# Four first expert blocks instead of three, three of them by seven products

## The chip, the cores and the metric

The kernel runs on one core of a Trainium2 chip. The metric is the device time of one execution in microseconds (us). Three runs of the kernel before gave 645.27, 646.94 and 648.63 us, so the median is 646.94 us. The profile is one further execution.

The engines are TensorE (PE in the profile, its weight loads PEld), VectorE (DVE), ScalarE (ACT), GpSimd (POOL) and SyncE (SP). SP issues the large loads, POOL the gathers and scatters by index.

## The reference

Attention with a causal sliding window of 64 over 8 sequences of 576 tokens, 8 heads of 64, is followed by a mixture of 8 experts with one expert per token:

```python
# x: attention output, (B, S, D) = (8, 576, 512); E = 8 experts; F = 1024
logits = x @ w_gate;  local = sigmoid(x @ w_local)
for b in range(B):
    prev = -1
    for s in range(S):
        fresh = argmax(logits[b, s])
        e = fresh if s == 0 or local[b, s] < 0.5 else prev
        prev = e
        p = softmax(logits[b, s])
        h = relu(x[b, s] @ w1[e])
        out[b, s] = p[e] * (h @ w2[e])
```

A token may take over the expert of the token before it, so the expert of a token is known only once the sequence has been scanned up to it.

## The kernel before, in words

**Attention** (`attention`, L167) goes through 9 chunks of 512 tokens (`sc`), each with 4 pairs of heads (`hp`): 36 units, written (sc, hp) here. A unit's scores (L377) are made two units ahead on PE, ACT takes the exponential (L415), and DVE multiplies by a mask (L420), but for the units in `BIASED`, where PE adds the mask as a bias. `values` (L423) multiplies with V on PE, and DVE scales (L440). The chunks 4 to 8 (`GATED`) get their gate logits beside the values. Each finished chunk is written to `xs` in DRAM by POOL (L532). Inside attention, PE, ACT and SP execute in the order in which the code is written; DVE's and POOL's order comes from a planner.

**Routing** (`Router`) works in two parts. The first (`first`, L986) takes the tokens up to `T1` = 3 sequences, finds each token's expert, and places tokens of full groups of 256 with one expert into `FB` = 3 first blocks. The second (`second`, L1019) takes the rest and builds the table of all further blocks. Both are generators, woven into other work: each `yield` gives a weight (the DVE work just written, in us) and a flag `trip`, which says that the next piece starts on PE with what DVE or ACT has just made. In attention a local `step` runs twice per unit and goes on when the weights, paid off at `HALF` per step, allow it. In the expert stage another `step` (L1441) pays off `STEP` = 3.5 per call.

The table (L938) is built from one-hot matrices, ten chunks of 128 tokens at a time: `one` and `colh` on DVE, `rowh` (in the second part) on ACT by an absolute value for each chunk (L964) and one relu (L966), then bfloat16 matmuls on PE (L972). The result gives the indices `gx` for the gathers. `weigh` (L883) writes each token's probability into a column of `xs` by DMAs on SP.

**Experts** (`Experts`) processes blocks of 256 tokens with one expert each, named -1, -2, -3 for the first blocks and 0, 1, ... for the further ones, with some smaller blocks between. Per block: a gather of rows (`rows`, L1130, on POOL), a load of `w1` and `w2` (`weights`, L1154, 2 MB each, on SP, into a ring of four buffers that attention's loads share), the transpose (`turn`, L1170), `hidden` and `result`. Blocks named in `PLAIN` (-1 and -2) use plain matmuls (L1375, L1407). All other large blocks use seven products in place of eight for each of the two matrix multiplications (`big_hidden` L1216, `big_result` L1268), for which DVE first makes sums of quarters: `xs` and `ws1` of input and `w1` (in `prepare`), `ws2` of `w2`, `hs` of the hidden layer. In such a block some results are read from a bank of PSUM that a later product adds into, so that product waits for the reader.

`run` (L1426) sets the order. PE and SP go in program order through the expert stage; DVE and ACT are left to the planner until block -3 is reached (L1481). Before block -3 the generator of the second part is emptied (L1476), the flag is made (L1479), and the next blocks are fetched by the new table.

Of the kernel before, what the change touches and what calls it, by code (L numbers as in the profile page):

```python
# [19 lines left out]
P = 128  # L20
# [6 lines left out]
N = B * S  # L27
# [9 lines left out]
T1 = 3 * S  # L37
CUT = T1 % P
PART = slice(0, T1 // P + 1), slice(T1 // P, C)
C1 = PART[0].stop  # L40
CV = C + 1
CMAX = max(p.stop - p.start for p in PART)
FB = 3
FIRST = 2 * FB
assert CUT and CUT % 32 == 0
# [10 lines left out]
ZR = 16 * P  # L56
# [13 lines left out]
HALF = 0.8  # L70
STEP = 3.5
LEAD = 2
MID = (KB, KB - 1)
PLAIN = (-1, -2)
# [92 lines left out]
def attention(ctx, tc, ring, kq, v3, v4, vt, vh, xs, lt, ok, wg, wg2, ident, rt, ex):  # L167
# [302 lines left out]
    for i, (sc, hp) in enumerate(units):  # L470
# [27 lines left out]
        if side is None and 4 * sc >= C1 and hp >= 2:  # L498
            side = rt.first(bank)
# [198 lines left out]
class Router:  # L698
# [18 lines left out]
    def prepare(self):  # L717
        nc = self.nc
        tl, iota = self.tl, self.iota
        self.io8 = iota("io8", [P, 1, E], [[0, 1], [1, E]])  # L720
        self.io8m = tl("io8m", P, 1, E)
        nc.vector.tensor_scalar(self.io8m, self.io8, -float(E), None, Alu.add)
        self.io128 = iota("io128", [P, 1, P], [[0, 1], [1, P]])
        self.ios = iota("ios", [P, 1, NS], [[0, 1], [1, NS]])
        self.iob = iota("iob", [1, NBLK, 1], [[1, NBLK], [0, 1]])
        pos = iota("pos", [P, G, GC], [[0, G], [P, GC]], 1)
        self.ones = tl("ones", P, P)
        nc.vector.memset(self.ones, 1.0)
        self.tri = tl("tri", P, P)
        nc.gpsimd.affine_select(out=self.tri, in_=self.ones, compare_op=Alu.is_gt, fill=0.0, base=0,  # L730
                                pattern=[[1, P]], channel_multiplier=-1)
        self.zero = tl("zero", P, CMAX * E)
        nc.vector.memset(self.zero, 0.0)
        self.begin = tl("begin", P, C)
        begin2 = tl("begin2", P, C)
        posf = pos.rearrange("p g c -> p (g c)")
        nc.vector.tensor_scalar(self.begin, posf, 0.0, None, Alu.is_equal)
        nc.vector.tensor_scalar(begin2, posf, float(S), None, Alu.is_equal)
        nc.vector.tensor_tensor(self.begin, self.begin, begin2, op=Alu.add)
        self.oh, self.rank = tl("oh", P, CV, E), tl("rank", P, CV, E)  # L740

        self.chunk = tl("chunk", P, CV, dt=BF16)
        for i, a in enumerate((0, C1)):
            c = PART[i]
            n = c.stop - c.start
            nc.vector.tensor_copy(self.chunk[:, a:a + n], iota(f"chunk{i}", [P, n], [[1, n]], 0, c.start - C))
        self.at = iota("posp", [P, 1], [[0, 1]], 1)
        self.cnt = [tl("cnt0", P, E), tl("cnt1", P, E)]
        self.lim1 = tl("lim1", P, E)
# [19 lines left out]
    def gate(self, part, psum):  # L769
# [75 lines left out]
        vec.memset(oh[:CUT, 0, :] if part else oh[CUT:, n - 1, :], 0.0)  # L845
# [37 lines left out]
    def weigh(self, part):  # L883

        chunks, xs = PART[part], self.xs
        c = chunks.start
        for a, b in ((0, T1), ) if not part else ((T1, ZR), (ZR, N)):
            for a, b in ((a, -(-a // P) * P), (-(-a // P) * P, b // P * P), (b // P * P, b)):
                if a >= b:
                    continue  # L890
                i, n, p = a // P, max(1, (b - a) // P), min(P, b - a)
                self.nc.sync.dma_start(
                    out=xs[row_of(a):row_of(a) + b - a, D:].rearrange("(c p) o -> p c o", p=p),
                    in_=self.pt[a % P:a % P + p, i - c:i - c + n])
# [7 lines left out]
    def places(self, pl, n):  # L902

        vec = self.nc.vector

        def tl(name, p, n, dt=F32):
            return self.tl(name, p, CV, dt=dt)[:, :n]

        plc = tl("plc", P, n)
        vec.tensor_reduce(plc, pl, axis=AX.X, op=Alu.add)  # L910

        vec.memset(plc[CUT:, C1 - 1:C1], float(2 * N))
        if n > C1:
            vec.memset(plc[:CUT, C1:C1 + 1], float(2 * N))
        plc_i = tl("plc_i", P, n, dt=I32)
        vec.tensor_copy(plc_i, plc)
        lo_i = tl("lo_i", P, n, dt=I32)
        vec.tensor_scalar(lo_i, plc_i, P - 1, None, Alu.bitwise_and)
        vec.tensor_scalar(plc_i, plc_i, P.bit_length() - 1, None, Alu.arith_shift_right)
        lo, hi = tl("lo", P, n), tl("hi", P, n)  # L920
        vec.tensor_copy(lo, lo_i)
        vec.tensor_copy(hi, plc_i)
        return lo, hi
# [14 lines left out]
    def table(self, psum, cs, ns, lo, hi, idx, gx):  # L938
# [5 lines left out]
        for k in range(0, len(pieces), 2):  # L944
            built = []
            for b, m in pieces[k:k + 2]:
# [15 lines left out]
                if ns != FIRST:  # L962
                    for i in range(m):
                        nc.scalar.activation(rowh[:, i, :], self.io128[:, 0, :], Act.Abs, bias=lo[:, b + i:b + i + 1],  # L964
                                             scale=-1.0)
                    nc.scalar.activation(rowh, rowh, Act.Relu, bias=self.ones[:, :1], scale=-1.0)  # L966
                yield 0.6 if ns == FIRST else 0.42 * m, (b, m) in (pieces[-1], pieces[k + 1:k + 2] and pieces[k + 1])
# [18 lines left out]
    def first(self, psum):  # L986
# [18 lines left out]
        pl = tl("pl", P, CV, E)[:, :C1]  # L1005
# [13 lines left out]
    def second(self, psum):  # L1019
# [55 lines left out]
        CE = [P, CV, E]  # L1075
# [16 lines left out]
        lo, hi = self.places(pl, CV)  # L1092
# [9 lines left out]
        at = yield from self.table(psum, slice(0, CV), NS, lo, hi, tabs["idx"], tabs["gx"])  # L1102
# [14 lines left out]
class Experts:  # L1117
# [52 lines left out]
    def turn(self, st, quiet, later=False):  # L1170
# [12 lines left out]
        if st["fast"] and not quiet and not later:  # L1183
            self.prepare(st)

    def prepare(self, st):

        st["xq"] = quarters(st["xt"], DK, BIG)
        st["xt"] = self.right("xs", st["xq"])
# [3 lines left out]
        st["ws"] = self.left("ws1", st["wq"])  # L1193

    def left(self, name, a):

        sub, add = Alu.subtract, Alu.add
        s1, s2, s3, s4 = self.sums(name, a)
        for o, x, y, op in ((s1, a[1][0], a[1][1], add), (s2, s1, a[0][0], sub), (s3, a[0][0], a[1][0], sub),
                            (s4, a[0][1], s2, sub)):  # L1200
            self.nc.vector.tensor_tensor(o, x, y, op=op)
        return s1, s2, s3, s4

    def right(self, name, b):

        sub = Alu.subtract
        t1, t2, t3, t4 = self.sums(name, b)
        for o, x, y in ((t1, b[0][1], b[0][0]), (t2, b[1][1], t1), (t3, b[1][1], b[0][1]), (t4, b[1][0], t2)):
            self.nc.vector.tensor_tensor(o, x, y, op=sub)
        return t1, t2, t3, t4  # L1210
# [5 lines left out]
    def big_hidden(self, st):  # L1216
# [9 lines left out]
        st["w2t"] = self.right("ws2", w2)  # L1226
# [22 lines left out]

        product(px, a[0][0], b[0][0], stop=False)  # L1250
        u = keep(0, px)
        product(py, s[0], t[0], stop=False)
        z = keep(1, py)
        product(px, s[1], t[1], False, False)
        v = keep(2, px)
        product(pz, a[0][1], b[1][0])
        relu(hq[0][0], pz, u)
        product(px, s[2], t[2], False, False)
        relu(hq[1][1], px, z)
        product(py, s[3], b[1][1], False)  # L1260
        relu(hq[0][1], py, v)
        product(px, a[1][1], t[3], False)
# [3 lines left out]
        st["hs"] = self.left("hs", st["ha"])  # L1266
# [94 lines left out]
    def hidden(self, st, quiet, step):  # L1361
        nc = self.nc
        if st["fast"]:
            return self.big_hidden(st)
# [3 lines left out]
        for g in range(FK // each):  # L1368
            hp = self.ps_h.tile([P, each, n], F32, name="hp")
            for i in range(each):  # L1370
                m = g * each + i
                for kk in range(DK):
                    for f in range(0, P, st["rows"]):
                        a = slice(f, f + st["rows"])
                        nc.tensor.matmul(hp[a, i, :], lhsT=st["w1"][:, kk, m * P:(m + 1) * P][:, a],  # L1375
                                         rhs=st["xt"][:, kk, :n], start=(kk == 0), stop=(kk == DK - 1))
            o = h[:, g * each:(g + 1) * each, :n]
# [4 lines left out]
            step()  # L1382

    def result(self, st, step, hooks=()):
# [3 lines left out]
        if "half" in st:  # L1388
# [13 lines left out]
            step()  # L1402
            return
        for i, s in enumerate(st["slots"]):
            yp = self.ps_y.tile([P, D], F32, name="yp")
            for m in range(FK):
                nc.tensor.matmul(yp, lhsT=st["h"][:, m, i * P:(i + 1) * P], rhs=st["w2"][:, m, :],  # L1407
                                 start=(m == 0), stop=(m == FK - 1))
                if m == FK // 2 - 1:
# [16 lines left out]
    def run(self, ctx, rt, last=None):  # L1426
# [4 lines left out]
        ctx.enter_context(tc.manual_schedule(engines={ET.PE, ET.SP}))  # L1431
# [7 lines left out]
        pause = 0.0  # L1439

        def step():  # L1441
            nonlocal side, pause
            pause -= STEP
            if pause > 0.0:
                return
            pause, trip = 0.6, False
            while side and not trip:
                w, trip = next(side, (0.0, None))
                pause += w
                if trip is None:  # L1450
                    side = None

# [18 lines left out]
        step()  # L1471
        pause += 2.0
        for i, n in enumerate(order):
            quiet = i < FB
            if i == FB - 1:
                while side:  # L1476
                    step()
                if last:
                    last(psum())  # L1479

                ctx.enter_context(tc.manual_schedule(engines={ET.PE, ET.SP, ET.DVE, ET.Activation}))  # L1481
                jobs.append(self.fetch(order[FB]))
                if jobs[i]["fast"]:
                    self.prepare(jobs[i])
# [4 lines left out]
            self.hidden(jobs[i], quiet, step)  # L1489
            if i + 1 == len(order):  # L1490
                self.result(jobs[i], step)
                continue
            self.turn(jobs[i + 1], i + 1 < FB)
            hooks = ()
            if order[i + 1] >= KINDS[2]:
                one, turned, two = self.quarter(jobs[i + 1])
                after = jobs[i + 2]
                hooks = one, turned, two, (lambda: None), (lambda: self.turn(after, False, True)), \
                    (lambda: self.prepare(after))
            self.result(jobs[i], step, hooks)  # L1500

    def more(self, ctx):

        self.space(ctx)
        for n in [*range(SURE[0], NB), *range(NB + SURE[1], NB + E), *range(KINDS[1] + SURE[2], KINDS[1] + E)]:
            st = self.fetch(n)
            self.turn(st, False)
            self.hidden(st, False, lambda: None)
            self.result(st, lambda: None)
# [54 lines left out]
```

## Time and profile before

| what | value |
|---|---|
| median of three runs | 646.94 us |
| profiled execution: time / span | 650.13 / 648.4 us |
| PE busy | 620.2 us (96%) |
| DVE / ACT / POOL busy | 386.3 / 199.9 / 130.7 us |
| attention | 0 to about 136 us |
| blocks -1 and -2, plain | 135.9 to 197.1 us |
| block -3, by seven products | 197.1 to 222.65 us |
| moved by DMA | 166.43 MB, mean 257 GB/s |

A line of the timeline has the start, the length, the engine, the line of the code, the operation, what it writes and reads, its shapes and its count; in brackets stands the idle time before it and what ended that. Neighbours of one kind are merged. A line of the table by windows has, for each engine, the busy time and the number of instructions. Matmul ends are modelled. PE's rows in fp32 count two records for each matmul that the code writes.

### The profile page before, as it was taken

The page shows a single profiled execution, that of the slowest core. Times are in us where ns is not written, and L with a number is a line of the kernel's source. Part 1 is how long each engine was busy: PE and PEld are TensorE (multiplying, and loading weights), DVE is VectorE, ACT ScalarE, POOL GpSimd, SP SyncE. Part 2 cuts the span into 40 slices and gives each one's busy share as a digit, 9 for nine tenths or more (in the row PEclk, how much of TensorE's full clock was granted, in tenths as well). Part 3 has the DMA queues.
Part 4 walks back from the last instruction along what each step waited for, and adds up shares of the span by engine and source line. Part 5 has one row for each costly group of instructions (what it writes and reads, how often), then busy time and mean ns, then how long its engine had stood idle before and what let it go on. Part 6 is the DMA issues. An engine that isn't in the chain of part 4 may idle for free. (4 is left out here: it accounts for less than half of the span.)

```text
span 648.4 us, 14791 instructions
## 1 busy us (share of the span) xinstructions
PE 620.2 (96%) x6319; PEld 536.8 (83%) x6319; DVE 386.3 (60%) x730; ACT 199.9 (31%) x364; POOL 130.7 (20%) x132
## 2 busy tenths in 40 slices
PE   8888997889999999999999999999999999999995
PEld 7777776775759999978998999887997998899994
DVE  6676578753964865364563683362917752886730
ACT  3766755611473122113120312021211221213120
POOL 5422112320002202111302220211312022111101
PEclk9999989999999999999999999999999999999999
DMA  8989999968745655586957565769768456856501
GB/s 331 418 340 343 379 351 370 362 212 361 212 146 213 231 225 187 197 314 253 381 215 259 226 235 221 251 238 365 252 248 317 167 204 251 342 172 231 192 17 38
DMA packets 26725, 166.43 MB, mean 257 GB/s; under 512 B 8163, under 2 KB 9209, under 8 KB 16666
## 3 DMA queue, kind: packets, MB, share of 16 engines
q1 hardware_dynamic: 17802, 135.53, 57.3%
q0 software_dynamic: 8848, 29.85, 11.8%
q8 instruction: 52, 0.85, 0.5%
q14 instruction: 23, 0.19, 0.1%
HBM read 146.18 MB, written 19.59 MB: 256 GB/s over the span
## 5 line engine op out<-in xcount | busy, mean ns | idle before, releaser
L1357 POOL DMA_INDIRECT out_dram<-y,idx x36 | 41.1, 1140 | 347.0 <-DVE y L1293 165.9
L1236 PE MATMUL hp<-xs,ws 128*128 128x128 f32 x672 | 79.6, 275 | 0.0
L1284 PE MATMUL hp<-ws,hs 128*128 128x256 f32 x336 | 77.6, 380 | 0.0
L1236 PEld LDWEIGHTS hp<-xs,ws 128*128 128x128 f32 x672 | 77.3, 192 | 0.0
L1284 PEld LDWEIGHTS hp<-ws,hs 128*128 128x128 f32 x336 | 63.5, 190 | 9.3 <-issue 0.8
L1375 PE MATMUL hp<-xt,w 128*64 128x64 f32 (+2 forms) x640 | 66.3, 276 | 0.9 <-issue 0.9
L1375 PEld LDWEIGHTS hp<-xt,w 128*128 128x128 f32 (+1 forms) x640 | 61.2, 170 | 5.9 <-issue 2.5
L1293 DVE SCALAR_TENSOR_TENSOR y<-hp,xg,kept 128x256 f32<-128x256 f32 x42 | 19.7, 481 | 71.4 <-issue 47.0
L1247 DVE TENSOR_TENSOR h<-hp,keep 128x512 f32<-128x512 f32 x42 | 28.7, 690 | 53.3 <-PE hp L1236 53.3
L1147 POOL DMA_INDIRECT xg<-xs,gx x40 | 48.7, 1217 | 44.7 <-issue 37.8
L1407 PE MATMUL yp<-w,h 128*128 128x512 f32 x128 | 56.6, 593 | 0.0
L1236 PEld LDWEIGHTS hp<-xt,w 128*128 128x128 f32 x448 | 53.2, 192 | 2.7 <-issue 1.3
L1236 PE MATMUL hp<-xt,w 128*128 128x128 f32 x448 | 54.7, 275 | 0.0
L1284 PE MATMUL hp<-w,h 128*128 128x256 f32 x224 | 53.6, 382 | 0.0
L430 PE MATMUL xo<-vb,p 128*64 128x74 f32 (+1 forms) x576 | 44.7, 230 | 8.5 <-issue 4.1
L415 ACT ACTIVATE p<-sp 128x512 f32<-128x512 f32 x72 | 39.2, 595 | 39.4 <-PE sp L384 37.3
L384 PEld LDWEIGHTS sp<-w 64*64 64x64 f32 x1296 | 38.7, 137 | 13.2 <-issue 9.9
L430 PEld LDWEIGHTS xo<-vb,p 128*64 128x64 f32 x576 | 39.0, 139 | 10.9 <-issue 4.8
L420 DVE TENSOR_TENSOR p<-p,mask 128x1024 f32<-128x1024 f32 x29 | 35.7, 1231 | 19.9 <-ACT p L415 19.8
L384 PE MATMUL sp<-w 64*64 64x128 f32 (+1 forms) x1296 | 43.7, 268 | 3.5 <-issue 2.4
L1284 PEld LDWEIGHTS hp<-w,h 128*128 128x128 f32 x224 | 41.3, 190 | 5.6 <-issue 0.4
L430 PE MATMUL xo<-va,p 128*64 128x74 f32 (+1 forms) x576 | 44.7, 230 | 0.8 <-issue 0.8
(280 smaller groups left out, 935.7 us busy)
## 6 DMA issues: line engine op xcount, KB each, us to landing
w<-in_w_dram SPq DMA_DIRECT2D x48, 2048.0 KB, 10.1
w<-in_kq_dram SPq DMA_DIRECT2D x17, 1024.0 KB, 10.4
xs<-x POOLq DMA_DIRECT2D x9, 1024.0 KB
va<-in_v_dram SPq DMA_DIRECT2D x5, 1184.0 KB
vtt<-in_vt_dram SPq DMA_DIRECT2D x5, 1024.0 KB, 6.8
va<-in_v_dram SPq DMA_DIRECT2D x3, 1040.0 KB, 8.9
va<-in_v_dram SPq DMA_DIRECT2D x2, 520.0 KB, 6.9
w<-in_kq_dram SPq DMA_DIRECT2D x2, 512.0 KB, 3.7
```

The source lines that it names most:

```text
L384: nc.tensor.matmul(sp[j][c * WIN:(c + 1) * WIN, a:b], lhsT=kt[h, hp, block * WIN:(block + 1) * WIN], rhs=qt[h, hp, a:b], start=not biased, ...
L415: nc.scalar.activation(p[:, j], sp[j], Act.Exp, scale=DH ** -0.5)
L420: masked.append(nc.vector.tensor_tensor(p, p, m.to_broadcast([P, 2, SC]), op=Alu.mult))
L430: nc.tensor.matmul(xo[par * WIN:(par + 1) * WIN, j, s * VW:s * VW + n], lhsT=p[:, j, b * WIN:(b + 1) * WIN], rhs=w[:, s, 2 * hp + j, :n], ...
L1147: self.nc.gpsimd.indirect_dma_start(out=x, out_offset=None, in_=self.xs[:rows, :], in_offset=bass.IndirectOffsetOnAxis(ap=gx[:, s:s + 1], ...
L1236: nc.tensor.matmul(out[:, m, :], lhsT=a[:, kk, m * P:(m + 1) * P], rhs=b[:, kk, :], start=start and m + kk == 0, stop=stop and (m, kk) == ...
L1247: nc.vector.tensor_tensor(o, x, y, op=add)
L1284: nc.tensor.matmul(out, lhsT=a[:, m, :], rhs=b[:, m, :], start=start and m == 0, stop=stop and m == FK // 2 - 1, skip_group_check=True)
L1293: nc.vector.scalar_tensor_tensor(y[i][:, j * w:(j + 1) * w], x, pw[i], y2, Alu.mult, Alu.add)
L1357: self.nc.gpsimd.indirect_dma_start(out=self.out[:, :], out_offset=bass.IndirectOffsetOnAxis(ap=st["idx"][:, s:s + 1], axis=0), in_=y, in_ ...
L1375: nc.tensor.matmul(hp[a, i, :], lhsT=st["w1"][:, kk, m * P:(m + 1) * P][:, a], rhs=st["xt"][:, kk, :n], start=(kk == 0), stop=(kk == DK - 1))
L1407: nc.tensor.matmul(yp, lhsT=st["h"][:, m, i * P:(i + 1) * P], rhs=st["w2"][:, m, :], start=(m == 0), stop=(m == FK - 1))
```

## The change

The first part of routing takes four sequences (2304 tokens, 18 whole chunks of 128), so that no chunk is shared by the two parts and the code for a shared chunk goes. There are four first blocks, and only -1 is plain; 12 further large blocks are certain instead of 13. The first part's generator starts once chunk 5 has begun, and attention's `step` pays off 1.0 instead of 0.8.

In the expert stage PE, SP, DVE and ACT are all in program order from the start. The generator of the second part now tells DVE work and ACT work apart and yields in smaller pieces, and `step(room)` pays off both: 1.7 and 1.7 per step in the plain block's hidden layer, 0.9 and 1.7 in its result, 0.5 and 1.4 in the blocks by seven products. The sums of the next block and of `w2` are handed out a few at a time at the same places. The generator is emptied before block -4.

```diff
-T1 = 3 * S
-CUT = T1 % P
-PART = slice(0, T1 // P + 1), slice(T1 // P, C)
+T1 = 4 * S
+PART = slice(0, T1 // P), slice(T1 // P, C)
-CV = C + 1
-FB = 3
+FB = 4
-ZR = 16 * P
+ZR = 20 * P
-HALF = 0.8
-STEP = 3.5
+HALF = 1.0
+HALFWAY, BESIDE, WITHIN = (1.7, 1.7), (0.9, 1.7), (0.5, 1.4)
-PLAIN = (-1, -2)
+PLAIN = (-1,)
...
-        if side is None and 4 * sc >= C1 and hp >= 2:
+        if side is None and 4 * sc >= C1 and (hp >= 2 or sc - 1 in GATED):
             side = rt.first(bank)
...
-                if ns != FIRST:
-                    for i in range(m):
-                        nc.scalar.activation(rowh[:, i, :], self.io128[:, 0, :], Act.Abs, bias=lo[:, b + i:b + i + 1],
-                                             scale=-1.0)
-                    nc.scalar.activation(rowh, rowh, Act.Relu, bias=self.ones[:, :1], scale=-1.0)
-                yield 0.6 if ns == FIRST else 0.42 * m, (b, m) in (pieces[-1], pieces[k + 1:k + 2] and pieces[k + 1])
+                trip = (b, m) in (pieces[-1], pieces[k + 1:k + 2] and pieces[k + 1])
+                if ns == FIRST:
+                    yield 0.6, trip
+                    continue
+                yield 0.17 * m, False
+                for i in range(m):
+                    nc.scalar.activation(rowh[:, i, :], self.io128[:, 0, :], Act.Abs, bias=lo[:, b + i:b + i + 1],
+                                         scale=-1.0)
+                    if i % 4 == 3:
+                        yield 0.0, False, 1.2
+                c = m // 2
+                nc.scalar.activation(rowh[:, :c], rowh[:, :c], Act.Relu, bias=self.ones[:, :1], scale=-1.0)
+                yield 0.0, False, 0.3 * (m % 4) + 0.7
+                nc.scalar.activation(rowh[:, c:], rowh[:, c:], Act.Relu, bias=self.ones[:, :1], scale=-1.0)
+                yield 0.0, trip, 0.7
...
+        def after():
+            if step:
+                self.do(more, 1)
+                step()
+        if not step:
+            self.do(more)
         product(px, a[0][0], b[0][0], stop=False)
         u = keep(0, px)
+        after()
         product(py, s[0], t[0], stop=False)
         z = keep(1, py)
+        after()
...
-        ctx.enter_context(tc.manual_schedule(engines={ET.PE, ET.SP}))
+        ctx.enter_context(tc.manual_schedule(engines={ET.PE, ET.SP, ET.DVE, ET.Activation}))
...
-        def step():
-            nonlocal side, pause
-            pause -= STEP
-            if pause > 0.0:
-                return
-            pause, trip = 0.6, False
-            while side and not trip:
-                w, trip = next(side, (0.0, None))
-                pause += w
+        def step(room):
+            nonlocal side, vector, scalar
+            vector, scalar = max(vector - room[0], -room[0]), max(scalar - room[1], -room[1])
+            while side and vector <= 0.0 and scalar <= 0.0:
+                w, trip, *busy = next(side, (0.0, None))
+                vector, scalar = vector + w, scalar + sum(busy)
                 if trip is None:
                     side = None
+                elif trip:
+                    vector += 0.3
+                    break
...
             if i == FB - 1:
                 while side:
-                    step()
+                    step(HALFWAY)
                 if last:
                     last(psum())
-                ctx.enter_context(tc.manual_schedule(engines={ET.PE, ET.SP, ET.DVE, ET.Activation}))
                 jobs.append(self.fetch(order[FB]))
...
-            self.hidden(jobs[i], quiet, step)
+            self.hidden(st, first, (lambda: step(WITHIN if st["fast"] else HALFWAY)) if i < FB - 1 else None)
...
-            self.turn(jobs[i + 1], i + 1 < FB)
+            after = jobs[i + 1]
+            self.turn(after, i + 1 < FB)
+            if i < FB - 1:
+                def beside():
+                    self.do(after["sums"], 2 if st["fast"] else 1)
+                    step(WITHIN if st["fast"] else BESIDE)
+                self.result(st, beside, [beside] * 6)
+                self.do(after["sums"])
+                continue
```

`do(terms, n)` writes the next `n` of a block's sums; `result` of a plain block calls its `step` four times per half, that of a block by seven products the six hooks between its products.

## The prediction

> **What bounds the kernel now.** I read the page first, then the stage table by windows, then the timelines of TensorE (PE), ScalarE (ACT), VectorE (DVE) and SyncE (SP) around the first expert blocks.
>
> ```profile
> PE 620.2 (96%) x6319; PEld 536.8 (83%) x6319; DVE 386.3 (60%) x730; ACT 199.9 (31%) x364; POOL 130.7 (20%) x132
> ```
>
> PE is busy 96% of the span, so a saving in matmuls counts, and so does every microsecond for which PE has to stand still. By stage (columns: window, then busy us and count of PE, PEld, DVE, ACT, POOL, then granted clock, DMA share, GB/s):
>
> ```profile
> 87.40:105.70 18.30, 15.74 (x398) 13.16 (x401) 15.71 (x62) 10.19 (x18) 3.16 (x3) 0.96 0.97 368
> 105.70:117.00 11.30, 9.86 (x258) 8.03 (x251) 8.14 (x20) 6.08 (x12) 3.27 (x3) 1.00 0.92 305
> 117.00:129.00 12.00, 11.20 (x302) 9.42 (x300) 9.95 (x24) 7.25 (x14) 4.07 (x3) 1.00 1.02 404
> ...
> 136.00:166.00 30.00, 30.00 (x114) 19.86 (x115) 14.63 (x68) 4.51 (x8) 5.76 (x6) 1.00 0.77 290
> 166.00:197.00 31.00, 30.64 (x142) 20.74 (x140) 23.88 (x64) 20.69 (x50) 2.58 (x3) 1.00 0.54 163
> 197.00:222.50 25.50, 25.50 (x177) 24.08 (x178) 15.45 (x34) 5.67 (x10) 5.20 (x6) 1.00 0.60 221
> ```
>
> Attention ends at 136. Two plain blocks follow (136 to 197), then fast blocks of 25.5 us. PE is never idle there, although DVE and ACT do the second routing part beside it. How it ends:
>
> ```profile
> 188.72 7.09 PE L1407 MATMUL yp<-w,h 128*128 128x512 f32 x16
> 195.65 0.99 PE L972 MATMUL r<-colh,rowh 128*128 128x108 bf16 x17
> 197.00 0.27 PE L160 MATMUL r<-ident,ok 128*1 128x128 f32 x1 [0.36 <-DVE t L974]
> 197.11 2.02 PE L1236 MATMUL hp<-xt,w 128*128 128x128 f32 x16
> ```
>
> PE passes from the second plain block to the third block in 1.46 us (195.65 to 197.11), as ACT had made the last one-hot rows beside the block's second result half:
>
> ```profile
> 188.54 3.31 ACT L964 ACTIVATE rowh<-io,lo 128x128 bf16<-128x128 f32 x11
> 191.75 1.35 ACT L966 ACTIVATE rowh<-rowh,ones 128x1280 bf16<-128x1280 bf16 x1
> 193.01 1.84 ACT L964 ACTIVATE rowh<-io,lo 128x128 bf16<-128x128 f32 x6
> 194.88 1.04 ACT L966 ACTIVATE rowh<-rowh,ones 128x896 bf16<-128x896 bf16 x1
> 195.85 0.69 ACT L1412 ACTIVATE y<-yp,xg 128x512 f32<-128x512 f32 x1
> ```
>
> The code writes these rows ahead of that half, so the block's last `y` (195.85) stands behind them and PE's wait is for a few matmuls alone.
>
> **The change part by part.** *Block -2 by seven products.* Sixteen large blocks remain (3 + 13 before, 4 + 12 after); one plain block becomes fast. Plain, from the PE timeline: hidden 13.81 (166.20 to 180.01), turn 0.87, results 6.87 and 6.93: 28.48. Fast: seven hidden products of 1.787, turn 0.87, seven result products of 1.726: 25.46. Gain **-3.0**.
>
> *The metering of the second part.* I walked the generator by its own weights. In the plain block every step pays off 1.7 or 0.9 us of DVE work, in blocks -2 and -3 only 0.5 (24 steps). The 7.2 chunk goes out at the seventh hidden step of block -1, the 7.4 chunk at its fifth result step, the first piece of the table only at the fourth result step of block -2. A piece then costs 1.7 of DVE at 0.5 per step and 4.1 of ACT at 1.4 per step, about six steps in turn; fifteen are left for four pieces. So at block -4 the loop that empties the generator still has: the ten rows of piece 3 on ACT, all of piece 4 (six rows), and the table's end.
>
> *The flush.* PE and ACT now go in program order. PE has the matmuls of pieces 3 and 4 and the transpose of `flag` ahead of block -4; ACT has block -3's last `y` ahead of the rows, and that waits for PE's last product. From that product's end: `y` 0.72 (starts 0.25 late, runs 0.47, as at 222.90), ten rows at 0.30 (eleven took 3.31) 3.0, two half activations of 640, 0.75 each (from 1.35 for 1280 and 1.04 for 896, overlap taken off) 1.5, six rows 1.8, two halves of 384 1.1: 8.1. Then six matmuls, the copy of the table and the flag, 1.05 (by 196.68 to 197.11): 9.15, against 1.46 before. **+7.7** (6.5 to 8.5). There is no cover: PE has nothing else in order.
>
> *The clock.* At 82 to 86 PE was idle for 1.54 of 4 us, and the granted clock was 0.87, 0.50 and 0.78 in the three windows of 2 us from 84 on, 1.7 us of clock lost in all; the 2.52 us idle at 101.8 to 104.3 cost none.
>
> ```profile
> 86.00:88.00 2.00, 2.00 (x35) 1.64 (x37) 1.49 (x6) 0.95 (x1) 0.00 (x0) 0.50 0.93 317
> 101.80:104.30 2.50, 0.00 (x1) 0.00 (x1) 2.50 (x7) 2.19 (x4) 0.00 (x0) 1.00 1.03 421
> ```
>
> Bounds for the flush 0 and 1.7; I take **+1.7**, as its 5 us of idle is twice the longest that passed unpunished. [...]
>
> *VectorE in program order, block -2.* Before, the 11.6 us from 161.64 to 173.2 held both chunks, two chains interleaved, small operations 0.08 to 0.1 apart; one behind the other they are 0.20 apart (118.15, 118.35, 118.55), so some 33 of them make it about 15. The matmuls of the one-hots come after the sixth hidden step, near 149; with 3.8 of counting, 15 of chunks and block -2's eight sums (6.1, as 184.01 to 190.15) DVE is through at 174, while PE starts block -2 at 167 (166.2 and the 0.9 below). Three `ws2` sums (1.14 each), a relu addition 0.65, the fourth sum and the second addition follow: 180. PE wants that addition before the seventh product, 167 + 6 x 1.787 = 177.7. With the semaphores' delays **+2.9** (0 to 5).
>
> *Waits inside the fast blocks.* At the fourth result hook of block -2 DVE gets two sums (2.28) and one piece's one-hots (1.74) between two `put`s: 0.43 + 2.28 + 1.74 + 0.43 = 4.9 after product 4, where the seventh product, which overwrites what the second `put` reads, comes after 3.45: +1.5. In hidden of -3 the same with one sum: 0.65 + 1.14 + 1.74 + 0.65 = 4.2 against 3.57: +0.6. In the result of -3 part is hidden by the table's matmuls: +0.3. **+2.4** (0 to 3.5).
>
> *First transposes of the second part.* They move from after the second group of block -1 (142.88) to after the first (139.4); `vk` was ready at 140.62. **+0.9** (0.3 to 1.5).
>
> *First part later.* Counting steps, it starts at (5,0) instead of (4,2) and ends at (7,2) instead of (7,1). Its DVE work before 87.4, 3.7 us, plus some 1.5 for 18 chunks instead of 14 comes on top of 33.8 busy in 41.6 us up to 129: 94%. The table's end, 118.84 before, moves one unit (3.1) to about 122. Behind it:
>
> ```profile
> 109.68 4.43 SPq L892 DMA_DIRECT2D xs<-ptw  x2
> 115.02 0.64 SPq L238 DMA_DIRECT2D late<-allr  x1
> 115.88 0.38 SPq L1163 DMA_DIRECT2D w<-in_w_dram  x1
> ```
>
> The weights' column (`ptw`) was issued ahead of the expert's `w1`; now its turn on SP comes at (6,3), behind the wait on `allr` and behind `w1` (2 MB). It starts near 114.7 and lands 8.5 to 10.7 later, 123 to 125, or up to 5 more if `w1` holds it. The gather of block -1 needs it: issue to 128, 8.5 to land, 136, where PE wanted the rows at 133.67. POOL also has two more gathers (1.3 each) before the first scatter; it was idle 15.6 us there, so nothing. **+3** (-2.1, if the idle of 71 to 87 goes and nothing comes, to +8).
>
> *At nothing:* the memsets (0.06) and DMAs that go; `weigh` of part 2 now waits on SP behind block -4's weights, whose buffer comes free at the end of block -2 near 195; landing takes 10.7, and its reader comes after the flush, 25 us later. Without that cover: 10.7. The gather for the next block stands to the flush as at 198.44.
>
> Sum: -3.0 + 7.7 + 1.7 + 2.9 + 2.4 + 0.9 + 3 = **+15.6**. The profiled execution (span 648.4, time 650.13) becomes 664 and 665.7; the runs' median, 646.94, is 3.2 below that time, so **662.5**.
>
> **The rivals.** *A, all of the side work is hidden.* If the last one-hot row on ACT is done before block -3's last product, and DVE keeps up, the waits of the expert stage vanish together: 646.94 - 3.0 + 3 = 646.9, not slower. For it: ACT was busy only 20.69 of 31 us while making all rows. Against it: the steps counted above. It decides at the start of block -4. *B, only the flush is hidden:* 662.5 - 9.4 = 653.1. *C, the start of block -1 sets the tone:* the gather is 5 us later still (DVE at 94%): 667.5. *D, DVE becomes the bound of blocks -2 and -3:* a fast block has 18.0 us of its own DVE work (222.6 to 248.1), so the two need 36, the backlog of 7 from block -1 and 6 for the pieces, 49 of 51 us. If order leaves a fifth of that as gaps, 58 are needed: +7, 669.5.
>
> **How the numbers follow.** Forecast 0.55, A 0.14, B 0.11, C 0.14, D 0.06. All lower ends give 648.6, all upper ones 672; without the outer ends and with B, C and most of D, 650 to 671; the forecast's own range is 655 to 669. A change of 0.5% (3.2 us) is what this measurement can tell from none. A is faster by that in 0.08 and about the same in 0.05; B is the same in 0.02: faster 0.08, same 0.07, slower 0.85.
>
> **What would show it.** Right: PE idle some 8 us before block -4, released by `rowh` on ACT, perhaps with the clock at 0.5 behind it; PE waiting on an `h` of DVE in block -2; `ptw` issued after `w1` and PE's first transpose of `xg` later than 134. Wrong: the table's last matmul ahead of block -3's end, or an attention that ends at 136 or before with its rows there.

## The result and the profile after

The changed kernel takes 669.45 us (median of four runs, 668.27 to 673.20), the kernel before 647.79 (median of four): a ratio of 1.0337 (95% interval 1.0265 to 1.0409). The change costs some 22 us. The profiled execution took 673.2 us, with a span of 671.3.

The page of the changed kernel, engines over the whole span, and its table by windows (columns as before: window, busy us and count of PE, PEld, DVE, ACT, POOL, granted clock, DMA share, GB/s):

```profile
PE 627.4 (93%) x6394; PEld 548.6 (82%) x6394; DVE 406.4 (61%) x743; ACT 203.1 (30%) x374; POOL 127.5 (19%) x131
```

```profile
147.00:178.20 31.20, 31.15 (x117) 20.30 (x116) 23.46 (x88) 4.36 (x8) 7.97 (x8) 0.98 0.78 297
178.20:210.00 31.80, 27.66 (x178) 25.69 (x177) 25.29 (x49) 7.49 (x13) 2.08 (x2) 0.95 0.49 163
210.00:238.20 28.20, 27.22 (x197) 24.85 (x195) 21.07 (x31) 15.35 (x37) 1.97 (x2) 1.00 0.51 162
238.20:247.00 8.80, 2.48 (x18) 1.37 (x18) 0.41 (x2) 7.58 (x21) 0.96 (x1) 0.64 0.59 227
```

The rows are block -1 (plain), -2, -3 (both by seven products) and the flush before block -4. Before, PE stood still beside the second part of routing for 0.36 us. Now it stands in block -2 for 4 us, and in the flush (the emptying of the generator, with PE waiting for its matmuls' inputs) it works 2.48 us of 8.8. PE's timeline shows what each wait was for (in brackets the idle time and what ended it):

```profile
142.97 1.94 PE L1172 MATMUL tp<-ident,xg 128*128 128x128 f32 x8 [5.29 <-DMA xg<-xs,gx]
...
191.70 2.77 PE L1243 MATMUL hp<-xs,w 128*128 128x128 f32 x16 [2.62 <-DVE h L1254]
208.16 1.99 PE L1305 MATMUL hp<-ws,h 128*128 128x256 f32 x8 [1.51 <-DVE y L1314]
221.54 2.05 PE L1243 MATMUL hp<-xs,w 128*128 128x128 f32 x16 [0.45 <-DVE h L1254]
236.40 2.00 PE L1305 MATMUL hp<-ws,h 128*128 128x256 f32 x8 [0.53 <-DVE y L1314]
242.59 1.35 PE L967 MATMUL r<-colh,rowh 128*128 128x108 bf16 x10 [4.20 <-ACT rowh L959]
245.56 0.96 PE L967 MATMUL r<-colh,rowh 128*128 128x108 bf16 x6 [1.62 <-ACT rowh L959]
246.88 0.37 PE L158 MATMUL r<-ident,ok 128*1 128x128 f32 x1 [0.36 <-DVE t L969]
```

The eight transposes at 142.97 take 1.94 us, and the seventh product at 191.70 takes 2.77 where undisturbed ones take 1.95: the clock is low behind these waits (granted 0.50 from 142.97 to 147.00, 0.69 from 191.70 to 194.70). Before, the same transposes took 1.09:

```profile
133.67 1.09 PE L1177 MATMUL tp<-ident,xg 128*128 128x128 f32 x8
```

ACT in the flush, every row behind block -3's last `y`:

```profile
238.43 0.47 ACT L1336 ACTIVATE y<-hp,xg 128x256 f32<-128x256 f32 x1 [6.65 <-PE hp L1305]
238.80 3.01 ACT L954 ACTIVATE rowh<-io,lo 128x128 bf16<-128x128 f32 x10
241.72 0.81 ACT L959 ACTIVATE rowh<-rowh,ones 128x640 bf16<-128x640 bf16 x1
...
243.16 1.85 ACT L954 ACTIVATE rowh<-io,lo 128x128 bf16<-128x128 f32 x6
```

SP, POOL and the list of DMA issues around the start of block -1 (the last line: kind, count, KB each, us from issue to landing):

```profile
121.35 0.36 SPq L1158 DMA_DIRECT2D w<-in_w_dram  x1
121.76 0.42 SPq L882 DMA_DIRECT2D xs<-ptw  x1
125.58 7.13 SPq L236 DMA_DIRECT2D late<-allr  x1
```

```profile
136.61 1.07 POOL L1142 DMA_INDIRECT xg<-xs,gx  x1 [14.22 <-DVE p L418]
```

```profile
xs<-ptw SPq DMA_DIRECT2D x1, 144.0 KB, 14.0
```

The row numbers `gx` were ready at 128.23, the column of weights landed at 121.76 + 14.0 = 135.8, and the gather started at 136.61. The line of POOL names an operation of DVE that had long been done, so the column is the better reading; the third run below names it outright.

By stage, from PE's timelines (us; "start" runs from SP's load of chunk 8's `vtt` to PE's wish for block -1's rows, "rows" from there to its first hidden matmul, "hidden -4" is the hidden layer of the block behind the flush; before, the flush stood ahead of block -3, which is counted whole, and 12.5 is the hidden layer of the block behind that one):

| | start | rows | -1 | -2 | -3 | flush | hidden -4 |
|---|---|---|---|---|---|---|---|
| before | 24.4 | 2.2 | 30.3 | 29.5 plain | 25.5 | 1.5 | 12.5 |
| after | 24.9 | 9.3 | 31.2 | 31.8 | 28.2 | 8.9 | 14.3 |
| more | 0.5 | 7.1 | 0.9 | 2.3 | 2.7 | 7.4 | 1.8 |

The last row sums to 22.7. Chunk 8's load was issued 3.5 us later in this execution (112.78 against 109.26), and the rest of the run was 3.3 shorter. The later start of that execution is not put down to the change: in the ten runs below that leave attention ahead of this load as the change has it (all but run 1), the load went out anywhere from 108.1 to 111.1. So 22.7 is what has to be explained, against 21.7 in the medians and 15.6 in the forecast.

### The profile page after: what moved, and what is told of

Read it like the earlier page. It is cut to its first block, busy times and chain, and to the rows that moved or that the text cites. A ratio compares the mean times of both kernels' runs of the same rounds, so it can differ in the third digit from the quotient of the medians.

```text
span 671.3 us, 14971 instructions
## 1 busy us (share of the span) xinstructions
PE 627.4 (93%) x6394; PEld 548.6 (82%) x6394; DVE 406.4 (61%) x743; ACT 203.1 (30%) x374; POOL 127.5 (19%) x131
## 5 line engine op out<-in xcount | busy, mean ns | idle before, releaser
L1243 PE MATMUL hp<-xs,ws 128*128 128x128 f32 x720 | 85.6, 276 | 0.0
L1243 PEld LDWEIGHTS hp<-xs,ws 128*128 128x128 f32 x720 | 83.1, 193 | 0.2 <-ACT keep L1249 0.2
L1305 PE MATMUL hp<-ws,hs 128*128 128x256 f32 x360 | 83.2, 380 | 0.0
L1209 DVE TENSOR_TENSOR ws<-w 128x1024 f32<-128x1024 f32 x60 | 73.3, 1221 | 7.6 <-PE hp L1305 7.6
L1243 PEld LDWEIGHTS hp<-xt,w 128*128 128x128 f32 x480 | 58.6, 197 | 3.2 <-issue 1.8
L1243 PE MATMUL hp<-xt,w 128*128 128x128 f32 x480 | 60.3, 280 | 0.0
L1209 DVE TENSOR_TENSOR ws<-w,ws 128x1024 f32<-128x1024 f32 x45 | 54.9, 1219 | 0.5
L1396 PE MATMUL hp<-xt,w 128*64 128x64 f32 (+2 forms) x576 | 53.1, 266 | 0.0
L1396 PEld LDWEIGHTS hp<-xt,w 128*128 128x128 f32 (+1 forms) x576 | 49.1, 169 | 2.6 <-issue 0.7
L1255 ACT ACTIVATE h<-h 128x512 f32<-128x512 f32 x45 | 28.1, 630 | 64.6 <-DVE h L1254 64.6
```

Of the source, the lines that this page charges most:

```text
L1209: return lambda: self.nc.vector.tensor_tensor(o, x, y, op=op)
L1243: nc.tensor.matmul(out[:, m, :], lhsT=a[:, kk, m * P:(m + 1) * P], rhs=b[:, kk, :], start=start and m + kk == 0, stop=stop and (m, kk) == ...
L1255: nc.scalar.activation(o, x if y is None else o, Act.Relu)
L1305: nc.tensor.matmul(out, lhsT=a[:, m, :], rhs=b[:, m, :], start=start and m == 0, stop=stop and m == FK // 2 - 1, skip_group_check=True)
```

## The experiments

Each kernel is the changed one with the edit shown. Ratios are to the kernel before in the same batch, whose median was 647.05 to 649.71 us.

**Run 1, the column at 101 us.** `weigh(0)` right behind `gate(0)`, as soon as the weights exist.

```diff
         yield from self.gate(0, psum)
+        self.weigh(0)
...
         yield 2.5, False
-        self.weigh(0)
```

> The changed kernel (669.5 us) with one edit: the first part's probabilities (ptw) are written by SP right after the first part's gating, so their place in SP's queue is ahead of chunk 8's last loads and of block -1's w1, where it was behind both. Theory 'the queue': block -1's rows were late (5.3 us of PE idle at 137.7) because the gather waited for this DMA, issued at 121.8 behind w1 and landed only at 136.6, while the indices were ready at 128.4. Then the gather starts near 129, the rows land near 136, PE's wait is 0 to 1 us, the clock stays up at block -1 (about 2 us more): 661 to 664. Rival 'the table': the rows are late because the first part's table is late (DVE full); then the gather still starts after 134 and at most 1 us is won: 668 to 670.

Measured: 666.52 us, 1.028 (1.0240 to 1.0319). The gather started at 126.33, 0.45 us after its row numbers, and PE's wait for the rows was gone. But attention now took 26.6 us from chunk 8's load, 1.7 more than after's. On SP the next load of attention, issued right behind the column, took 9.15 us to issue:

```profile
101.22 0.39 SPq L882 DMA_DIRECT2D xs<-ptw  x1
101.65 9.15 SPq L230 DMA_DIRECT2D w<-in_kq_dram  x1
```

The queue theory holds for the gather, and the rival, a late table, falls: the row numbers were there at 125.88. The time still lies between both expectations, since attention took back part of what the gather gave.

**Run 2, wider metering in the fast blocks.** The side work gets more room per step.

```diff
-HALFWAY, BESIDE, WITHIN = (1.7, 1.7), (0.9, 1.7), (0.5, 1.4)
+HALFWAY, BESIDE, WITHIN = (1.7, 1.7), (0.9, 1.7), (0.9, 2.1)
```

> The changed kernel with one edit: in blocks -2 and -3 each step pays off 0.9 us of DVE and 2.1 of ACT work instead of 0.5 and 1.4. By the count of the steps the generator is then empty before block -3 ends. Theory 'metering': the stretch from block -3's last product to block -4's first falls from 8.9 to under 1 us and the clock at block -4 stays at 1.0 (1.8 us): 659 to 662, with the waits in blocks -2 and -3 changed by no more than 1.5 us. Rival 'it only moves': DVE and ACT have no time for it inside the two blocks, so the waits there grow by 6 us or more: 666 or above.

Measured: 660.61 us, 1.0195 (1.0169 to 1.0220), as expected. The flush is gone, and with it the low clock behind it: block -4's first product takes 1.95 us in place of 3.62.

```profile
235.64 1.99 PE L1305 MATMUL hp<-ws,h 128*128 128x256 f32 x8 [1.21 <-DVE y L1314]
237.47 0.27 PE L158 MATMUL r<-ident,ok 128*1 128x128 f32 x1
237.58 1.95 PE L1243 MATMUL hp<-xt,w 128*128 128x128 f32 x16
```

Blocks -2 and -3 got longer instead, 33.3 and 29.3 us; the wait for DVE before block -2's seventh product was still there (2.90 us), the product behind it took 3.78 us in place of 1.95 and the transposes after that 1.91 in place of 1.04, and all 36 matmuls of the table now lie in block -3. So the flush was a matter of metering; DVE's waits were not.

**Run 3, DVE and ACT left to the planner until block -4**, as it was before the change up to block -3.

```diff
-        ctx.enter_context(tc.manual_schedule(engines={ET.PE, ET.SP, ET.DVE, ET.Activation}))
+        ctx.enter_context(tc.manual_schedule(engines={ET.PE, ET.SP}))
...
                     last(psum())
+                ctx.enter_context(tc.manual_schedule(engines={ET.PE, ET.SP, ET.DVE, ET.Activation}))
```

> The changed kernel with one edit: DVE and ACT are left to the planner until block -4, as the kernel before has it until its block -3; PE and SP in program order, all else as changed. Theory 'program order': with the planner two chains are interleaved on DVE and the one-hot rows can run early on ACT, so the DVE backlog in block -2 (2.8 us and 1.7 us of PE idle) goes, and the 8.9 us before block -4 shrink to 2 to 4: 655 to 661. Rival 'the written order is what counts': PE's own order and the places where the generator is advanced fix the stall, the planner changes nothing there: 667 to 671.

Measured: 657.48 us, 1.0157 (1.0121 to 1.0193), as expected. Blocks -2 and -3 took 26.8 and 26.5 us, the flush 3.0. The start of block -1 was untouched, and here POOL's gather names what it waits for:

```profile
133.31 1.07 POOL L1142 DMA_INDIRECT xg<-xs,gx  x1 [14.04 <-DMA xs<-ptw]
```

**Run 4, two plain blocks**, as before the change: `PLAIN = (-1,)` becomes `(-1, -2)`.

> The changed kernel with one edit: block -2 is plain again (four first blocks, two of them plain). Theory 'cover': block -2 by seven products saves 3.0 us of matmuls but takes the steps away in which the second part was done; plain, it costs 3.0 us, and the flush before block -4 (7.4 us over the old 1.5, and 1.8 of clock), the waits in block -2 (2.8 + 1.7) and the low clock behind them (about 1.9) go: 655 to 659. Rival 'the conversion pays': the flush and waits come from elsewhere; 671 to 673.

Measured: 655.05 us, 1.0120 (1.0075 to 1.0165). With a plain block beside the table, program order brings no wait in blocks -2 and -3 (30.2 and 25.7 us, all 36 matmuls of the table in -2) and no flush. What stays is the start of block -1: 5.28 us of wait for the rows, 9.3 us to the first hidden matmul.

**Run 5, the column between chunk 8's loads and `w1`**, at 111 us, the place it had on SP before the change.

```diff
         if (sc, hp) == (NSC - 3, 3):
+            rt.weigh(0)
             ex.jobs = [ex.weights({}, -1, ("w1",), lambda: until(2, allr[:1, sc, hp, 0, :1]))]
...
         yield 2.5, False
-        self.weigh(0)
```

> The column of weights (ptw, 144 KB in 2,304 rows of 64 B) is issued on SP after the last load of attention's chunk 8 (about 113 us) and ahead of block -1's w1, in place of behind w1 at 117 to 122. Queue theory (the gather of block -1 waits for the landing of the column, and the column was late because of its place on SP): it lands by 121 to 127, the gather starts with its row numbers at 125 to 128, the 5.2 us wait of the first transposes and the low clock behind it (about 2 us) go, attention's own loads are not touched: 662 to 664 us against 669.5. The loads of w1 and w2 come up to 8 us later, which block -1 does not feel. Rival (the run with the column at 101 us: attention gets longer by what the wait gives back, wherever the column is put): 666 to 669 us.

Measured: 667.09 us, 1.0260 (1.0214 to 1.0306). The gather started at 126.26, "rows" fell from 9.3 to 2.7 us, and SP's next issue was not slowed (0.63 us). Yet "start" grew from 24.9 to 28.5 us: the rival's outcome, without the cause it named, as no load of attention stood behind the column here.

**Runs 6 and 7, this column with the cures of the expert stage.** Run 6 adds the two plain blocks, run 7 the planner and the wider metering.

> Two blocks plain (655.05 us) and the column between chunk 8's loads and w1. If the two causes are separate, the sum is 655.05 less 6 to 7.5 = 647.5 to 649 us, level with the kernel before, and nothing of the change's cost is left unnamed. If the start of block -1 waits for something else too, 651 to 655 us.

> VectorE and ScalarE left to the planner until block -4 (657.48 us), the wider metering inside fast blocks (it took the last 3 us of the flush away), and the column between chunk 8's loads and w1; block -2 stays on seven products. Separate causes: 657.48 - 3 - 6 to 7.5 = 647 to 648.5 us; the conversion's 3 us then show as 0 to 1 us against the kernel with two plain blocks. If the wider metering brings waits back into blocks -2 and -3 even with the planner: 650 to 652 us.

Measured: run 6 653.29 us, 1.0043 (1.0013 to 1.0072); run 7 650.52 us, 1.0021 (0.9999 to 1.0043). On the 647.87 us that the expectations stood on, run 6 is 650.7, 1.7 above the upper end of what was expected, and run 7 649.2, 0.7 above. Run 7 is level with the kernel before. In both, attention was longer again ("start" 28.4 and 27.4). DVE's timeline of run 7 says why:

```profile
130.43 0.23 DVE L436 TENSOR_TENSOR g<-xo,allr 128x72 f32<-128x72 f32 x1
133.58 0.69 DVE L438 TENSOR_TENSOR x<-xo,allr 128x512 f32<-128x512 f32 x1 [2.91 <-DMA xs<-x]
```

Chunk 8's outputs want one of two buffers back, and the write of that buffer's rows to `xs` (1 MB), issued by POOL at 117.00, had not landed. Runs 1, 5 and 6 show the same wait, of 2.35, 2.06 and 3.37 us; after's own trace has none. The difference is on SP: in runs 1 and 5 to 7 block -1's `w2` is issued at 121.9 to 124.2, some 5 us after that write (6.5 before the change, without a wait), while in the changed kernel the slow issue behind the column held it back to 132.99, 11.4 us after the write. The write and `w2` in run 7, and `w2` in after:

```profile
117.00 0.75 POOL L531 DMA_DIRECT2D xs<-x  x1 [3.58 <-DVE x L438]
121.88 0.34 SPq L1158 DMA_DIRECT2D w<-in_w_dram  x1
```

```profile
132.99 0.99 SPq L1158 DMA_DIRECT2D w<-in_w_dram  x1
```

If this reading is right, the column's lateness had kept another transfer out of the way; runs 9 and 10 put it to the test.

**Run 8, dummies in the two waits.** PE is kept at work by transposes that nothing reads.

```diff
+        fill(36)
         self.turn(jobs[0], True)
...
             if i == FB - 1:
+                fill(30)
                 while side:
```

> The changed kernel with transposes of the identity that nothing reads: 36 ahead of block -1's first transposes and 30 ahead of the flush, so that TensorE works (about 0.136 us each, 4.9 and 4.1 us) while it would idle 5.3 and 4.2 us. No wait of the two is shortened. Clock theory (the idle time closes the clock, and the work behind it runs slow): block -1's transposes 1.1 in place of 1.9 us, hidden product of block -4 12.5 in place of 14.3 us, the whole 665 to 667 us. Rival (what follows is slow for other reasons, such as transfers or ScalarE): 669 to 671 us.

Measured: 665.78 us, 1.0265 (1.0223 to 1.0307). At block -1 the theory holds: from the first transposes to the first hidden matmul 2.1 us in place of 4.0, at a granted clock of 1.00 in place of 0.50. At the flush it fails in its size: hidden -4 took 13.8 us, not 12.5. The windows of run 8 (the second begins at the dummies' end):

```profile
228.80:232.30 3.50, 3.46 (x31) 3.20 (x29) 0.00 (x0) 3.28 (x11) 0.00 (x0) 1.00 0.92 371
232.30:237.50 5.20, 1.62 (x17) 0.98 (x18) 0.42 (x2) 4.31 (x11) 0.11 (x1) 0.94 0.36 147
237.50:240.50 3.00, 3.00 (x16) 3.00 (x16) 2.73 (x15) 0.00 (x0) 1.87 (x2) 0.54 0.23 87
```

The remaining waits, 3.6 us within 5.2, were followed by a clock of 0.54, without the first wait. So at block -1 the clock is shown to be the cost behind the wait. The time lies where the clock theory had it, but not by the dummies alone: the clock also stayed at 1.00 behind block -2's wait, some 1.6 us that they did nothing for. The length of the idle time alone does not tell: 2.65 us had no low clock behind it here and 2.67 us had one in run 10, as the last section shows.

**Runs 9 and 10, `w2` two units later.** Run 9 is run 7 with it, run 10 is run 5 with it.

```diff
-        if (sc, hp) == (NSC - 2, 1):
+        if (sc, hp) == (NSC - 2, 3):
             ex.weights(ex.jobs[0], -1, ("w2",), lambda: until(3, allr[:1, sc, hp, 0, :1]))
```

> The kernel of the planner, the wider metering and the column between (1.0021 of the kernel before), with block -1's w2 issued two units of attention later (about 127 in place of 122 us). Contention theory: there VectorE's last x waited 2.9 us for the write of chunk 6's rows (1 MB, issued at 117.0, landing 16 us later beside w1, w2 and the gathers), TensorE waited 2.0 us for that and ran at 0.9 of its clock around it. With w2 behind the write, the wait and the low clock go: 2 to 4 us less, 0.996 to 0.999 of the kernel before. Rival (the write is slow by itself or by the gathers, w2 makes no difference): 1.001 to 1.003.

> The changed kernel with the column between chunk 8's loads and w1 (1.026 of the kernel before), and block -1's w2 two units later; nothing else. Contention theory: the 2.1 us wait of VectorE for the write of rows and the low clock behind it go, 3 us less: 1.020 to 1.022; what is left are the flush (7.4 + 1.8 us) and the waits of block -2. Rival: 1.025 to 1.027.

Measured: run 9 647.37 us, 0.9986 (0.9969 to 1.0002); run 10 662.90 us, 1.0241 (1.0210 to 1.0272). In both traces `w2` goes out over 10 us after the write, the wait for the write is gone, and PE goes from attention into block -1 without a pause ("start" 24.0 and 23.9, "rows" 2.2). Run 9's `w2` on SP (the write went out at 119.89) and its DVE, at the place of run 7's wait, and run 10's PE:

```profile
130.63 0.34 SPq L1158 DMA_DIRECT2D w<-in_w_dram  x1
```

```profile
132.44 0.23 DVE L436 TENSOR_TENSOR g<-xo,allr 128x72 f32<-128x72 f32 x1
132.59 0.68 DVE L438 TENSOR_TENSOR x<-xo,allr 128x512 f32<-128x512 f32 x1
```

```profile
132.16 1.09 PE L1172 MATMUL tp<-ident,xg 128*128 128x128 f32 x8
```

In time, run 9 gained 0.35% on run 7, as the contention theory had it. Run 10's 1.0241 lies between the two expectations: its gain on run 5, 0.2%, is less than half of what was expected, and by its interval could be nothing, where the traces say 4.6 us in "start". Against after, run 10 is 1.0% faster, some 6 us; the two traces put the start of block -1 at 8.1 us ("start" and "rows", 34.2 and 26.1).

**Run 11, DVE alone left to the planner.** ACT stays in program order.

```diff
-        ctx.enter_context(tc.manual_schedule(engines={ET.PE, ET.SP, ET.DVE, ET.Activation}))
+        ctx.enter_context(tc.manual_schedule(engines={ET.PE, ET.SP, ET.Activation}))
...
                     last(psum())
+                ctx.enter_context(tc.manual_schedule(engines={ET.PE, ET.SP, ET.DVE, ET.Activation}))
```

> The changed kernel with VectorE alone left to the planner until block -4; ScalarE stays in program order. Prediction's attribution (the waits in blocks -2 and -3 come from VectorE's order, the flush from ScalarE's order and the metering): the 2.6 and 1.5 us waits of block -2 and the low clock behind them go (4 to 6 us), the flush stays at 8.9 us with 4.2 us of wait on ScalarE's rows: 1.022 to 1.027 of the kernel before, against 1.034 for the change and 1.016 with both engines left to the planner. Rival (ScalarE's order, which holds block -2's relus and copies too, makes these waits; or VectorE's order makes the flush): waits of over 1.5 us stay in block -2, 1.030 to 1.034, or the flush shrinks to 3 us, 1.016 to 1.018.

Measured: 663.44 us, 1.0210 (1.0191 to 1.0229), a little under the attribution's lower end. Every wait inside blocks -2 and -3 went (25.7 and 26.7 us), and the flush stayed to the hundredth:

```profile
226.32 1.89 PE L1305 MATMUL hp<-ws,h 128*128 128x256 f32 x8
232.41 1.35 PE L967 MATMUL r<-colh,rowh 128*128 128x108 bf16 x10 [4.20 <-ACT rowh L959]
235.39 0.95 PE L967 MATMUL r<-colh,rowh 128*128 128x108 bf16 x6 [1.62 <-ACT rowh L959]
```

So DVE's order makes the waits inside the blocks, and ACT's order with the metering makes the flush: two separate causes, which the forecast had kept apart in the same way. ACT alone was not freed in any run; its part follows from runs 3 and 11 together.

## Why the prediction was right or wrong, point by point

The direction held. The range, 655 to 669, held only just: the ratio puts 668.7 on the 646.94 us that the forecast stood on, and the median itself, 669.45, is above its end. The time came out 6 to 7 us above the forecast. Against 15.6 stood 22.7 in the traces.

- **Conversion of block -2, -3.0.** Right. By seven products and without waits it takes 25.67 us (run 11); plain it takes 30.23 with the table's 36 matmuls (run 4), which are 1.8, so 28.4: 2.8 won.
- **Flush, +7.7.** Right: +7.4, with ACT's rows in the order and with the lengths that were walked. Run 2 shows the metering as its origin, run 11 that DVE's order has no part in it.
- **Clock behind the flush, +1.7.** Right in after's trace, +1.8.
- **DVE's backlog in block -2, +2.9.** Right: 2.62 us before the seventh hidden product, at the instruction that was named, gone with DVE's program order (run 11).
- **Waits inside the fast blocks, +2.4.** Right: 1.51, 0.45 and 0.53, together 2.5, for 1.5, 0.6 and 0.3.
- **First transposes of the second part, +0.9.** Right in size, in after's trace partly by luck: block -1 is 0.9 us longer, but what shows there is the low clock at its start (0.63 over the first 2 us, 0.7 lost), and `vk` came ready meanwhile. The forecast's wait for `vk` stands by itself where the matmuls ahead of it were not slowed (3.72 us for the first 16 records, 4.43 in after), 0.76 us in run 4 and 0.75 in run 10. Run 8, whose block -1 began later behind its rows, has neither and takes 30.2.
- **First part later, +3 (-2.1 to +8).** Mis-sized: "start" and "rows" together are 7.6 us longer, near the upper end. The step that failed is the column's place on SP, "It starts near 114.7 and lands 8.5 to 10.7 later, 123 to 125, or up to 5 more if `w1` holds it". It cannot start ahead of a `w1` that itself went out at 115.88 before; it went at 121.76 (118.2 if that execution's late start of 3.5 us is taken off), and took 14.0 us to land. The table was not the cause: `gx` was ready at 128.23, 8.4 us ahead of the gather. Also, the step let the price be the wait alone, while 1.8 us of low clock followed 5.3 of idle; the forecast priced the clock at the flush and not here.
- **Left out: the clock behind the 2.62 us wait of block -2.** Some 1.6 us: with the same two waits block -2 takes 31.8 us in after and 30.2 in run 8, where the clock stayed at 1.00. The forecast put nothing behind this wait and gave no reason; its row of 2.52 us of idle time without a loss shows one case, not a rule.

Of the rivals, A and B fell: the table ends behind block -3. C, a gather 5 us later still, is what came about at block -1, on top of the forecast's flush and waits; it had a chance of 0.14, its time of 667.5 is 2 us short, and it came through the column on SP and not through DVE "at 94%". D's size is near, by luck: its time is 669.5, and it gave the two fast blocks 58 us, where they took 60.0, of which 1.0 are matmuls of the table and 1.6 clock. But DVE was no bound there (46.4 of 60.0 us busy); freeing its order alone removes the waits (run 11).

Behind the flush 1.8 us of clock were lost (14.3 us for the hidden layer in place of 12.5), as the forecast's sum had it, and not nothing, as by its row at 101.8.

Where did the gain of the conversion go? Part of it is there in the trace of run 9, whose stages from "start" to the flush take 111.6 us against 113.4 before, 1.8 less. All else that the change brought, 22.7 + 3 us, was in the main three places: the flush and its clock (9.2), DVE's waits and their clock (6.7), and the start of block -1 (7.6); the rest is small terms. Each could be removed by itself (runs 2, 11 and 10), though run 2 gave some of it back inside the blocks; with all removed (run 9) the kernel is level with the one before, not measurably faster.

## What to carry to other kernels

Side work that a planner had laid into the gaps of an engine has to be paid by a meter once that engine goes in program order; what the meter has not paid by the next dependence is a flush at full price (here 7.4 us), with the clock's price on top (1.8). When a DMA moves on a queue, ask both who waits for its landing and which later transfers it was holding back: here the late column kept `w2` off the write of rows (11.4 us behind it in place of some 5), and curing the one uncovered the other (waits of 2.06 to 3.37 us for that write in runs 1 and 5 to 7). Look up the place of the DMA ahead of which the moved one is claimed to go; one line of the trace before would have shown that the column could not leave before `w1`.

## What the runs showed of the hardware that was not expected

**Behind the column of small pieces the next issue on SP took up to 9.15 us.** 144 KB in 2,304 pieces of 64 B took 0.42 us to issue (after, run 3), but the next DMA on SP took 7.13 us (after) and 7.41 (run 3) when it began 3.8 us behind the column's start, and 9.15 (run 1) when it began 0.4 us behind it. In after and run 3 that next DMA moves next to nothing (0.0 KB in the list of DMA issues). Where the next began 7.3 us behind (runs 5 and 7) it took 0.63; and with `w1` alone 4.4 us ahead of it, in the kernel before, 0.66. What the loads of 1 or 2 MB beside the column add to this is not separated here. The landing took 11.3 us at 101 (run 1) and 13.8 to 14.0 beside `w1`; before the change the second part's column, 160 KB, took 10.7.

**An idle time of 2.62 to 2.67 us was followed by a low clock in four executions and not in a fifth.** The wait before block -2's seventh product lasted 2.62, 2.64, 2.65, 2.67 and 2.65 us in after, run 5, run 1, run 10 and run 8. The product behind it took 2.77, 2.55, 3.66, 2.64 and 2.05 us, and the clock granted over 3 us from its start was 0.69, 0.73, 0.51 (in run 1 from 0.6 us later), 0.71 and 1.00. Run 10 and run 8, the 3 us behind the wait:

```profile
179.10:182.10 3.00, 3.00 (x19) 3.00 (x20) 2.27 (x4) 1.53 (x3) 0.00 (x0) 0.71 0.00 0
```

```profile
184.00:187.00 3.00, 3.00 (x26) 2.97 (x27) 2.27 (x4) 2.12 (x4) 0.00 (x0) 1.00 0.08 16
```

DVE is alike in the two, ACT nearly so (1.53 and 2.12 us busy), and the DMA engines are all but idle; the granted clock is 0.71 and 1.00. What decides is not visible in these traces. A wait of this length has to be priced with a loss of clock that may or may not come.
